# Threshold attention and a bilinear feed-forward layer: five more units of weights turned on TensorE

## The chip, the cores and the metric

The kernel runs on one core of a Trainium2 chip. The metric is the device time of one execution in microseconds (us); less is better. The time before is the median of three runs. A profiled execution, taken by the hardware profiler, shows every instruction of the engines: PE (TensorE's matmuls; PEld its weight loads), DVE (VectorE), ACT (ScalarE), POOL (GpSimd) and SP (SyncE, which issues nearly all DMAs here). Each engine works through its own instructions strictly in the order in which the program has them.

## What is computed

Attention over 8 batches of 8 heads, 576 rows and 64 columns a head, in which only scores within `tau` of their row's maximum count; the heads are put side by side to 4608 rows of 512, and these go through a bilinear layer with 1536 hidden columns.

```python
scores = scale * np.matmul(q, k.transpose(0, 1, 3, 2))
thresh = np.max(scores, axis=-1, keepdims=True) - tau
scores = np.where(scores >= thresh, scores, -1000000000.0)
scores = scores - np.max(scores, axis=-1, keepdims=True)
attn = np.exp(scores)
attn = attn / (np.sum(attn, axis=-1, keepdims=True) + 1e-09)
x = np.matmul(attn, v)                  # (B,H,S,D) -> (B*S, H*D)
out = (x @ w_a) * (x @ w_b) @ w_out
```

All of it is in float32, for which TensorE makes two passes for each matmul; the profile counts passes.

## The kernel before, in words

**Units and slots.** Heads are taken in pairs: a batch has four pairs (0 to 3). A unit `(i, u)` is 128 rows of scores for each head of pair `i` (u = 0 to 3), or, with u = 4 (`NT`), the 64 rows left over of each head, for two neighbouring pairs together. Batch 0 has 18 units: eight of the first half ((0,0) to (3,0), (0,1) to (3,1)), then ten of the second half: 8 = (0,2), 9 = (0,3), 10 = (0,4), 11 = (1,2), 12 = (1,3), 13 = (2,2), 14 = (2,3), 15 = (2,4), 16 = (3,2), 17 = (3,3). There are 144 units in all. The main loop (line 991) has one slot `g` for each, and all instructions of a slot are written out in a fixed order, kept by `keep_order`.

**What a slot does for its unit.** `scores` (line 374): 8 matmuls into two pairs of PSUM banks (line 388), the row maxima on DVE (395) and a threshold (396). `weigh` (406): exponentials on ACT (415, 416), then on DVE the masking with row sums (419); after that the two pairs of banks are free. `reciprocal` (424): while weights are still being converted, the 1e-9 is added on ACT (428) and DVE takes the reciprocal (432).

**Turning.** The products with v need the weights with keys on the partitions. Up to unit 7 (`BY_PE = 8`) TensorE does it: ACT writes two diagonal matrices of reciprocals (`diagonals`, 446), and in the next slot `turn_pe` multiplies the weights, piece by piece, by the diagonals (463; 18 matmuls with 128 moving columns), into two pairs of banks, from which ACT (465) and DVE (466) copy to `wT`. The product (`weighted_unit`) follows two slots after the scores. From unit 8 on ACT scales the weights (`normalise`, 438), DVE turns 32x32 blocks (`turn_blocks`, 482), SP's queue writes them to a DRAM tile `swap` and reads them back in another order into `wT` (`turn_back`, 505), and the product (`weighted`, 590) follows three slots after the scores (`PV_LAG`), for two units of a pair at once. Because the blocks lie in another order, v of batch 0 is loaded a second time (line 1088).

**Feed-forward work.** When a half of 256 rows is complete for all pairs, a generator (`ffn`, line 739) gives its matmuls (691, 764 and 821 or 867) in small steps; `advance(cols)` puts so many columns of them into a slot at fixed places. The speed is set by `PACE`, or by what is left until the next half arrives (line 1012). Each product of a hidden block and w_a or w_b fills a pair of banks (`pab`); ACT copies the first out (770), DVE multiplies the second in (772).

**PSUM.** There are four pairs of banks (`banks`, line 128) for scores, turned weights (`tp`), products with v (`pv`) and the feed-forward layer (`pab`, `po`). A matmul that takes a pair of banks waits until the engine that read its former content is done.

**Weight conversion.** The weights of the layer arrive as 64-bit words. Up to slot 15 each slot converts two or three pieces: ACT (288, 289), POOL (295), then a slot later DVE (301, 309) and POOL (314). In DVE's order one conversion follows the maxima, and one or two follow the reciprocal; in ACT's order the pair 288, 289 of the slot's first piece comes ahead of line 428.

Of the kernel before, what the change touches and what calls it, by code (L numbers as in the profile page):

```python
# [22 lines left out]
PV_LAG = 3  # L23
BY_PE = 8
# [30 lines left out]
def kernel(  # L55
# [411 lines left out]

    def parts(i, u):

        if i < HP:  # L470
            return {1: [(i, 0)], 3: [(i, 1)], NT: [(i, 2), (i + 1, 2)]}.get(u, [])
        return {1: [(i, 0)], NT if i % 2 == 0 else 3: [(i, 1)]}.get(u, [])
# [117 lines left out]
    def weighted(i, h):  # L590
# [4 lines left out]
        if h < 2:  # L595
            groups = G + (n > HALF)
            wT = [turned.pop((i, 2 * h + y))[:, 0:groups] for y in range(2)]
        else:
            t = turned[i - i % 2, NT]
            wT = [t[:, i % 2 * 2 + y:i % 2 * 2 + y + 1] for y in range(2)]  # L600
            if i % 2:
                del turned[i - 1, NT]
        pv = product([lambda rows, s, t=t: t[rows, :, s] for t in wT], loaded[i]["v"], n)
# [374 lines left out]

    def convert_rest(g, k):

        for n in early.get(g - 1, [])[k:k + 1]:
            convert_sign(n)
            convert_shift(n)
            convert_add(n)

    n = 0
# [4 lines left out]
    for g in range(len(units) + PV_LAG):  # L991
# [7 lines left out]
        back = ()  # L999
        if BY_PE + 1 < g <= len(units) + 1:  # L1000
            n = g - PV_LAG
            back = (1 if BY_PE <= n and parts(*units[n]) else 0,)
            if not back[0]:
                turn_back(*units[g - 2])
# [5 lines left out]
        pace = (PACE if g > BY_PE else PACE_EARLY) * BLOCK_COLS  # L1010
        if g > BY_PE:
            pace = min(pace, backlog() / (min([a for a in arrivals if a > g] + [len(units) + PV_LAG + 1]) - g))
        pace += NSLOT * S / (2 * NT + 1) + CATCH_UP * max(backlog() - BLOCK_COLS, 0)
        if 2 <= g < BY_PE + 2:
            weighted_unit(*units[g - 2])
            running["owed"] -= NSLOT * P // 2
# [12 lines left out]
        if g > BY_PE:  # L1029
            advance(PORTIONS[0] * pace)  # L1030
        for p in range(HP, NPR):
            for name, d in (("q0", 1), ("q1", 1)):
                if g == (second if name == "q1" else first)[p] - d - (name == "q1" and p % 2):
                    prep(p, name)
        if here:
            weigh(i, u)
        if here and g < BY_PE:
            reciprocal(i, u, nc.vector)
        if 0 < g <= BY_PE:
            turn_pe(*units[g - 1])  # L1040
        if g < 3:
            prep_copy(*prep_pe(g + 1, "k"))
# [4 lines left out]
        if g > BY_PE:  # L1047
            n = g - PV_LAG
            held = 0.0
            now = parts(*units[n]) if BY_PE <= n < len(units) else []  # L1050
            if now:
                held = 384 - (PORTIONS[2] + PORTIONS[3]) * pace + NSLOT * sum(width(*x) for x in now) // 2
                held = min(max(held, 0.0), 384)
            advance(PORTIONS[1] * pace - held)
            for p, h in now:
                if pairs[p][1] == 0:
                    make_x(2 if h == 1 and p >= HP and pairs[p][0] % GT == 0 else 1)
                make_room()
                weighted(p, h)
                passed(NSLOT * width(p, h) // 2)  # L1060
                running["owed"] -= NSLOT * width(p, h) // 2
            if back and back[0] > 0:
                turn_back(*units[g - 2])
# [3 lines left out]
        if here and g < BY_PE:  # L1067
            diagonals(i, u)
        elif here:
            reciprocal(i, u, nc.scalar if converting else nc.vector)  # L1070
            normalise(i, u)
        convert_rest(g, 1)
        if g <= BY_PE:
# [13 lines left out]
        if BY_PE <= g < BY_PE + HP:  # L1087
            load_v(g - BY_PE, again=True)
        store(written)
        if g > BY_PE:  # L1090
# [58 lines left out]
```

## Time and profile before

| | before |
|---|---|
| median of three runs | 1430.13 us (1428.39 to 1431.39) |
| span of the profiled execution | 1425.2 us |
| PE busy | 1369.9 us (96%), 34208 passes |
| DVE busy | 1007.7 us (71%) |
| ACT busy | 679.4 us (48%) |
| POOL busy | 480.7 us (34%) |

The span is the time from the first to the last instruction of the profiled execution. The page of the profile cuts it into 40 equal slices of 35.6 us; each digit is the busy share of a slice in tenths, PEclk the granted clock of TensorE:

```profile
PE   6778999999999999999999999999999999999998
DVE  6899887788777877776767767677777776744323
ACT  5787554545445454545444545454545455431010
PEclk9999999999999999999999999999999999999999
```

PE is below nine tenths in the first four slices alone (0 to 142 us), where DVE is at its busiest. The groups of instructions that the change touches, with busy us and the mean of one in ns, then the idle time of their engine just before them:

```profile
L438 ACT ACTIVATE tw<-tw,rcp 128x576 f32<-128x576 f32 x272 | 196.1, 768 | 198.1 <-DVE rcp L432 198.1
L482 DVE STREAM_TRANSPOSE tw<-tw 128x576 f32<-128x576 f32 x272 | 194.4, 752 | 0.8 <-ACT tw L438 0.8
L526 PE MATMUL pv<-wT,vm 64*64 64x160 f32 (+3 forms) x5184 | 170.8, 274 | 6.8 <-DMA wT<-swap 3.3
L465 ACT COPY wT<-tp x16: 575/589/599, 22.5 to 83.0; 128x512 f32<-128x512 f32 x16
```

The last line, from the view of one line's instructions, gives the shortest, the median and the longest of them in ns, and when the first and the last began.

### The profile page before, as it was taken

The numbers are of one execution on the slowest core, as the hardware profiler recorded it, in microseconds if no ns is written. First come the engines' busy times: TensorE is split into PE (matmuls) and PEld (weight loads), VectorE is DVE, ScalarE is ACT, GpSimd is POOL, SyncE is SP. The second block draws the span as 40 slices with busy tenths as digits, with TensorE's granted clock in tenths as the row PEclk, the third lists the DMA queues.
The fourth block names the chain that finished last, engine by engine and source line by source line (L and its number), as shares of the span: only waits on it lengthen the run. The fifth ranks groups of instructions, "written<-read, shape, count | busy, mean of one in ns | idle before, by whom it ended". The sixth has DMA issues, their size and how long they took to land.

```text
span 1425.2 us, 76956 instructions
## 1 busy us (share of the span) xinstructions
PE 1369.9 (96%) x34208; PEld 1237.2 (87%) x34208; DVE 1007.7 (71%) x2196; ACT 679.4 (48%) x1244; POOL 480.7 (34%) x668
## 2 busy tenths in 40 slices
PE   6778999999999999999999999999999999999998
PEld 5677689999978887988999989988898899799998
DVE  6899887788777877776767767677777776744323
ACT  5787554545445454545444545454545455431010
POOL 2674541606060605042333323241515060605000
PEclk9999999999999999999999999999999999999999
DMA  9977785667657775666546766567655775550000
GB/s 208 230 220 200 173 220 156 183 146 199 183 141 185 185 184 151 177 156 183 142 130 152 186 171 175 132 174 181 183 135 145 194 196 151 131 151 18 3 18 17
DMA packets 327003, 223.25 MB, mean 157 GB/s; under 512 B 171536, under 2 KB 310800, under 8 KB 326672
## 3 DMA queue, kind: packets, MB, share of 16 engines
q1 hardware_dynamic: 324160, 217.74, 59.6%
q8 instruction: 269, 4.41, 1.4%
q10 hardware_dynamic: 2512, 0.59, 0.2%
q14 instruction: 62, 0.51, 0.1%
HBM read 128.58 MB, written 89.65 MB: 153 GB/s over the span
## 4 chain that ended last, share of the span: by engine, by line
PE 83%; DVE 6%; DMA 5%; SPq 3%; issue 2%; ACT 1%; DVEq 0%; ACTq 0%
PE pab L691 27%; PE po L821 21%; PE pab L764 17%; PE pv L526 10%; PE sc L388 9%; SPq L143 2%; DVE mx L395 1%; DVE tw L482 1%; DMA vm<-in_v_dram 1%; DMA wT<-swap 1%; DVE tw L419 1%; DMA qT<-in_q_dram 1%; DMA sums_u<-in_moe_w_b_dram 1%; DMA raw<-in_moe_w_a_dram 1%; SPq L266 0%
## 5 line engine op out<-in xcount | busy, mean ns | idle before, releaser
L395 DVE TENSOR_REDUCE mx<-sc 128x1 f32<-128x576 f32 x288 | 204.6, 752 | 128.4 <-PE sc L388 127.4
L438 ACT ACTIVATE tw<-tw,rcp 128x576 f32<-128x576 f32 x272 | 196.1, 768 | 198.1 <-DVE rcp L432 198.1
L416 ACT ACTIVATE tw<-sc,bias,scalars 128x576 f32<-128x576 f32 x288 | 239.6, 832 | 10.9 <-DMA qT<-in_q_dram 0.4
L657 POOL TENSOR_TENSOR h<-h,u 128x512 f32<-128x512 f32 x28 | 35.1, 1274 | 605.2 <-DVE h L734 425.8
L419 DVE SCALAR_TENSOR_TENSOR tw<-sc,thr,tw 128x576 f32<-128x576 f32 x288 | 221.4, 799 | 10.0 <-ACT tw L416 9.3
L821 PE MATMUL po<-wo_sb,h 64*64 64x256 f32 x3264 | 208.3, 376 | 1.2 <-DVE h L734 1.1
L482 DVE STREAM_TRANSPOSE tw<-tw 128x576 f32<-128x576 f32 x272 | 194.4, 752 | 0.8 <-ACT tw L438 0.8
L821 PEld LDWEIGHTS po<-wo_sb,h 64*64 64x64 f32 x3264 | 157.7, 133 | 26.5 <-DVE h L734 2.6
L526 PEld LDWEIGHTS pv<-wT,vm 64*64 64x64 f32 x5184 | 160.7, 135 | 19.5 <-issue 11.1
L526 PE MATMUL pv<-wT,vm 64*64 64x160 f32 (+3 forms) x5184 | 170.8, 274 | 6.8 <-DMA wT<-swap 3.3
L388 PE MATMUL sc<-kT,qT 64*64 64x288 f32 x2016 | 168.5, 405 | 2.2 <-DVE xt L534 1.6
L821 PE MATMUL po<-sums_u,h 64*64 64x256 f32 x2448 | 155.1, 376 | 0.7 <-DVE h L772 0.7
L790 POOL TENSOR_TENSOR h<-h 128x256 f32<-128x256 f32 x168 | 117.3, 731 | 107.7 <-PE po L821 102.8
L821 PEld LDWEIGHTS po<-sums_u,h 64*64 64x64 f32 x2448 | 117.2, 133 | 21.3 <-DVE h L772 1.7
L691 PE MATMUL pab<-xU,wb_sb 64*64 64x128 f32 x4096 | 132.6, 269 | 0.0
L691 PEld LDWEIGHTS pab<-xU,wb_sb 64*64 64x64 f32 x4096 | 127.5, 133 | 2.8 <-ACT h L716 0.6
L388 PEld LDWEIGHTS sc<-kT,qT 64*64 64x64 f32 x2016 | 102.2, 134 | 22.8 <-issue 4.9
L415 ACT ACTIVATE bias<-mx,scalars 128x1 f32<-128x1 f32 x288 | 82.8, 287 | 69.0 <-DVE mx L395 68.6
L533 ACT COPY xT<-pv 128x128 f32<-128x128 f32 (+1 forms) x68 | 17.7, 260 | 204.9 <-PE pv L526 204.8
L534 DVE COPY xT<-pv 64x128 f32<-64x128 f32 (+1 forms) x136 | 38.2, 281 | 92.3 <-PE pv L526 90.8
L764 PE MATMUL pab<-xS,wa_sb 64*64 64x256 f32 (+1 forms) x1536 | 99.3, 363 | 0.0
L691 PE MATMUL pab<-xS,wa_sb 64*64 64x128 f32 x2048 | 96.5, 269 | 0.4 <-issue 0.4
(138 smaller groups left out, 2366.2 us busy)
## 6 DMA issues: line engine op xcount, KB each, us to landing
wT<-swap SPq DMA_DIRECT2D x244, 288.0 KB, 4.0
swap<-tw SPq DMA_DIRECT2D x480, 144.0 KB, 3.1
vm<-in_v_dram SPq DMA_DIRECT2D x128, 72.0 KB, 2.3
swap<-tw SPq DMA_DIRECT2D x128, 72.0 KB, 3.0
kT<-in_k_dram SPq DMA_DIRECT2D x112, 72.0 KB, 3.5
wT<-swap SPq DMA_DIRECT2D x56, 144.0 KB, 3.6
out_dram<-kept SPq DMA_DIRECT2D x30, 256.0 KB, 4.1
qT<-in_q_dram SPq DMA_DIRECT2D x112, 40.0 KB, 3.0
```

Of the source, the lines that this page charges most:

```text
L388: nc.tensor.matmul(sc[m][o * D:(o + 1) * D, c], qT[r, q0:q0 + D], kT[r, c * SH:(c + 1) * SH], start=True, stop=True)
L395: nc.vector.tensor_reduce(mx[:, c], sc[j], axis=AX.XY, op=ALU.max)
L415: nc.scalar.activation(bias[:, j:j + 1], mx[:, j:j + 1], AF.Copy, scale=e_nscale)
L416: nc.scalar.activation(wb[j], sb[j], AF.Exp, bias=bias[:, j:j + 1], scale=e_scale)
L419: nc.vector.scalar_tensor_tensor(out=wv, in0=sb[j], scalar=thr[:, j:j + 1], in1=wv, op0=ALU.is_ge, op1=ALU.mult, accum_out=sums[:, j:j + 1])
L438: nc.scalar.activation(w, w, AF.Copy, scale=rcp[:, j:j + 1])
L482: nc.vector.transpose(w, w)
L526: nc.tensor.matmul(pv[c * D:(c + 1) * D, y], vm[rows, s], wT[y](rows, s), start=(s == 0), stop=(s == NSLOT - 1))
L691: nc.tensor.matmul(out[c * D:(c + 1) * D, r, f * P:(f + 1) * P], w[g][k][rows, w0:w0 + D], moving[k][rows], start=(fresh and k == 0 and f ...
L764: nc.tensor.matmul(pab[c * D:(c + 1) * D, r], w[rows, f // n, k, fs + c * D:fs + (c + 1) * D], moving, start=(k == 0), stop=(k == H - 1))
L790: (nc.vector if state["over"] else nc.gpsimd).tensor_tensor(*a, **kw)
L821: nc.tensor.matmul(po[c * D:(c + 1) * D, r, y], ht[rows, t0:t0 + D], other[rows, f], start=(f == 0), stop=(f == NF // 2 - 1))
```

## The change

Units 8 to 12, which are the second halves of pairs 0 and 1 and the leftover rows of both, are turned by TensorE as well. `BY_PE` becomes 13; what began after unit 7 before, and has to do with the feed-forward pace and with `turn_pe` itself, now hangs on a new constant `ALONE = 8`. For these five units ACT writes diagonals in place of scaling the weights, and DVE's transposes, the writes to `swap`, the reads into `wT` and the second load of v for pairs 0 and 1 fall away.

The new `turn_part` takes a unit in two parts, each into one pair of banks that ACT copies out in one instruction (128x640 and 128x512). For an ordinary unit the parts have 8 matmuls with 128 moving columns and 4 with 64, and 8 with 128; for unit 10 they have 20 and 16 with 64. The first part stands after `weigh`, the second after the second portion of feed-forward work. `place` says where a piece lies in `wT`, and `turned_of` hands the product its columns.

The products of units 8 to 12 come two slots after the scores and not three (`weigh_out(now)`, in slots 10 to 14), and stand ahead of `weigh` in their slot. The feed-forward pace counts the turning still to come in these slots (`turns`).

```diff
@@ -21,7 +21,9 @@
     return struct.unpack("<f", struct.pack("<I", bits))[0]
 
 PV_LAG = 3
-BY_PE = 8
+ALONE = 8
+BY_PE = 13
+PE_PAIRS = 2
 XT_BUFS = 7
 Q_BUFS = 2
 OSB_BUFS = 4
@@ -465,6 +467,45 @@
             nc.scalar.copy(wT[:, y * NT:(y + 1) * NT], tp[:, y])
         nc.vector.tensor_copy(wT[:, 2 * NT], last[:, 0])
 
+    def place(s, o):
+
+        if s == 2 * NT:
+            return 2 * P + D + o * (2 * P + D) - D
+        if s >= NT:
+            return 2 * (2 * P + D) + (s - NT) * P + o * D
+        return s // 2 * (2 * P + D) + s % 2 * P + o * D
+
+    def turn_part(i, u, n):
+
+        if n == 0:
+            ws, dg = weights.pop((i, u))
+            t = turned_tile()[:, 0:G].rearrange("p g s e -> p (g s e)")
+            turned[i, u] = [t, [w.rearrange("p n e -> p (n e)") for w in ws], dg]
+        t, ws, dg = turned[i, u]
+        c0, width = ((0, 2 * P + D), (2 * (2 * P + D), 2 * P))[n]
+        tp = banks(width, "tp")
+        for s in ((0, 1, 2, 3, 8), (4, 5, 6, 7))[n]:
+            each = [(0, P)] if u < NT and s < 2 * NT else [(0, D), (1, D)]
+            for o, m in each:
+                y, c = divmod(place(s, o) - c0, width)
+                for j in range(2):
+                    w, d = (j, o * D) if u < NT else (o, (j ^ o) * D)
+                    nc.tensor.matmul(tp[j * D:(j + 1) * D, y, c:c + m], ws[w][:, s * D:(s + 1) * D],
+                                     dg[:, w, d:d + m], start=True, stop=True)
+        nc.scalar.copy(t[:, c0:c0 + 2 * width].rearrange("p (y w) -> p y w", y=2), tp)
+        if n:
+            turned[i, u] = t
+
+    def turned_of(t, o=None, c0=0, n=P):
+
+        def columns(rows, s):
+            if o is None:
+                if s < 2 * NT:
+                    return t[rows, place(s, 0):place(s, 0) + P]
+                return t[rows, 0:2 * (2 * P + D)].rearrange("p (y w) -> p y w", y=2)[:, :, 2 * P:]
+            return t[rows, place(s, o) + c0:place(s, o) + c0 + n]
+        return columns
+
     def parts(i, u):
 
         if i < HP:
@@ -592,15 +633,21 @@
         b, hp = pairs[i]
         flush(("v", i), ("wT", i if i >= HP or h < 2 else i - i % 2, h))
         n = width(i, h)
-        if h < 2:
+        if i >= PE_PAIRS and h < 2:
             groups = G + (n > HALF)
             wT = [turned.pop((i, 2 * h + y))[:, 0:groups] for y in range(2)]
+            wT = [lambda rows, s, t=t: t[rows, :, s] for t in wT]
+        elif h < 2:
+            wT = [turned_of(turned.pop((i, 2 * h + y))) for y in range(2)]
         else:
             t = turned[i - i % 2, NT]
-            wT = [t[:, i % 2 * 2 + y:i % 2 * 2 + y + 1] for y in range(2)]
+            if i < PE_PAIRS:
+                wT = [turned_of(t, i % 2, y * Q, Q) for y in range(2)]
+            else:
+                wT = [lambda rows, s, t=t[:, i % 2 * 2 + y]: t[rows, s] for y in range(2)]
             if i % 2:
                 del turned[i - 1, NT]
-        pv = product([lambda rows, s, t=t: t[rows, :, s] for t in wT], loaded[i]["v"], n)
+        pv = product(wT, loaded[i]["v"], n)
         read = [], []
         settled_of[i] = settled_of.get(i, 0) + n
         if settled_of[i] == S:
@@ -976,6 +1023,16 @@
     nc.vector.tensor_tensor(cut, cut, big, op=ALU.add)
     early = {}
 
+    def weigh_out(now):
+
+        for p, h in now:
+            if pairs[p][1] == 0:
+                make_x(2 if h == 1 and p >= HP and pairs[p][0] % GT == 0 else 1)
+            make_room()
+            weighted(p, h)
+            passed(NSLOT * width(p, h) // 2)
+            running["owed"] -= NSLOT * width(p, h) // 2
+
     def convert_rest(g, k):
 
         for n in early.get(g - 1, [])[k:k + 1]:
@@ -996,22 +1053,24 @@
         state["converted"] = state["added"]
         here = g < len(units)
         converting = bool(early.get(g)) or bool(early.get(g - 1))
-        back = ()
+        n = g - (2 if g < BY_PE + 2 else PV_LAG)
+        now = parts(*units[n]) if ALONE <= n < len(units) and not (g >= BY_PE + 2 and n < BY_PE) else []
+        back = False
         if BY_PE + 1 < g <= len(units) + 1:
-            n = g - PV_LAG
-            back = (1 if BY_PE <= n and parts(*units[n]) else 0,)
-            if not back[0]:
+            back = bool(now)
+            if not back:
                 turn_back(*units[g - 2])
         if here:
             i, u = units[g]
             scores(i, u)
             passed(S)
         exchange_blocks()
-        pace = (PACE if g > BY_PE else PACE_EARLY) * BLOCK_COLS
-        if g > BY_PE:
-            pace = min(pace, backlog() / (min([a for a in arrivals if a > g] + [len(units) + PV_LAG + 1]) - g))
+        pace = (PACE if g > ALONE else PACE_EARLY) * BLOCK_COLS
+        if g > ALONE:
+            turns = max(BY_PE - g + 1, 0) * NSLOT * P
+            pace = min(pace, (backlog() + turns) / (min([a for a in arrivals if a > g] + [len(units) + PV_LAG + 1]) - g))
         pace += NSLOT * S / (2 * NT + 1) + CATCH_UP * max(backlog() - BLOCK_COLS, 0)
-        if 2 <= g < BY_PE + 2:
+        if 2 <= g < ALONE + 2:
             weighted_unit(*units[g - 2])
             running["owed"] -= NSLOT * P // 2
         if g < 3:
@@ -1026,51 +1085,53 @@
         load_weights(RAWS)
         if g > BY_PE and g <= len(units):
             turn_blocks(*units[g - 1])
-        if g > BY_PE:
+        if g > ALONE:
             advance(PORTIONS[0] * pace)
+        if g < BY_PE + 2:
+            weigh_out(now)
         for p in range(HP, NPR):
             for name, d in (("q0", 1), ("q1", 1)):
                 if g == (second if name == "q1" else first)[p] - d - (name == "q1" and p % 2):
                     prep(p, name)
         if here:
             weigh(i, u)
-        if here and g < BY_PE:
+        if here and g < ALONE:
             reciprocal(i, u, nc.vector)
-        if 0 < g <= BY_PE:
+        if 0 < g <= ALONE:
             turn_pe(*units[g - 1])
+        elif ALONE < g <= BY_PE:
+            make_room()
+            turn_part(*units[g - 1], 0)
+            running["owed"] -= 5 * P
         if g < 3:
             prep_copy(*prep_pe(g + 1, "k"))
         for p in range(HP, NPR):
             for name, d in (("k", 2),):
                 if g == (second if False else first)[p] - d:
                     prep(p, name)
-        if g > BY_PE:
-            n = g - PV_LAG
+        if g > ALONE:
             held = 0.0
-            now = parts(*units[n]) if BY_PE <= n < len(units) else []
-            if now:
+            if now and g >= BY_PE + 2:
                 held = 384 - (PORTIONS[2] + PORTIONS[3]) * pace + NSLOT * sum(width(*x) for x in now) // 2
                 held = min(max(held, 0.0), 384)
             advance(PORTIONS[1] * pace - held)
-            for p, h in now:
-                if pairs[p][1] == 0:
-                    make_x(2 if h == 1 and p >= HP and pairs[p][0] % GT == 0 else 1)
+            if g >= BY_PE + 2:
+                weigh_out(now)
+            if back:
+                turn_back(*units[g - 2])
+            if g <= BY_PE:
                 make_room()
-                weighted(p, h)
-                passed(NSLOT * width(p, h) // 2)
-                running["owed"] -= NSLOT * width(p, h) // 2
-            if back and back[0] > 0:
-                turn_back(*units[g - 2])
+                turn_part(*units[g - 1], 1)
+                running["owed"] -= 4 * P
         for n in early.get(g, [])[:1]:
             convert_first(n)
             convert_clamp(n)
-        if here and g < BY_PE:
-            diagonals(i, u)
-        elif here:
-            reciprocal(i, u, nc.scalar if converting else nc.vector)
-            normalise(i, u)
+        if here:
+            if g >= ALONE:
+                reciprocal(i, u, nc.scalar if converting else nc.vector)
+            (diagonals if g < BY_PE else normalise)(i, u)
         convert_rest(g, 1)
-        if g <= BY_PE:
+        if g <= ALONE:
             advance(pace)
         convert_rest(g, 2)
         for n in early.get(g, [])[1:]:
@@ -1084,10 +1145,10 @@
         for p in range(1, NPR):
             if g == first[p] - 1:
                 load_v(p)
-        if BY_PE <= g < BY_PE + HP:
-            load_v(g - BY_PE, again=True)
+        if PE_PAIRS <= g - ALONE < HP:
+            load_v(g - ALONE, again=True)
         store(written)
-        if g > BY_PE:
+        if g > ALONE:
             if held:
                 owed, running["owed"] = running["owed"], 0.0
                 advance(held)
```

## The prediction

> **What bounds the kernel now.** I read the span in large stretches first, then slot by slot (a slot runs from one unit's first score matmul, line 388, to the next one's), then the instructions of the slots that the change touches. All times count from the start of the profiled span.
>
> The stretches (columns: length, then busy us and instructions of PE, PEld, DVE, ACT, POOL, then granted clock, DMA share, GB/s):
>
> ```profile
> 88.16:159.31 71.15, 63.02 (x1585) 53.70 (x1581) 66.34 (x144) 52.22 (x102) 41.45 (x42) 0.98 0.78 199
> 159.31:209.14 49.83, 45.71 (x844) 35.59 (x843) 39.28 (x88) 25.47 (x46) 23.16 (x15) 0.97 0.80 200
> 209.14:1253.57 1044.43, 1032.89 (x26207) 929.64 (x26201) 771.56 (x1694) 516.32 (x931) 347.68 (x518) 1.00 0.64 167
> ```
>
> From 209 us on PE is busy 1032.9 of 1044.4 us at full clock: the kernel is matmul-bound there, and one us of matmul added or of idle removed earlier shifts the end by one us. Slots 9 to 17 (88.16 to 159.31) are different: DVE is busy 66.3 of 71.2 us, PE 63.0. These are the slots in which the change works.
>
> What a slot costs PE at its best I take from undisturbed rows: 8 score matmuls 0.97 us; 32 passes with 128 moving columns 0.87, with 256 columns 1.73; a product of line 526 with 64, 128 or twice 32 columns 1.2, 1.96, 2.1; the 36 passes of line 463 2.19. Slots 24 and 25 last 9.41 and 7.01 us and add up to 9.41 and 7.02, so the prices hold. Slots 9 to 22 then lose, as duration less sum, 1.9, 4.5, 2.1, 0, 2.6, 0.9, 0.4, 0, 1.0, 4.0, 0.7, 1.0, 0.1, 1.0: 20.1 us. That is all there is to win here.
>
> PE about slot 10, the largest loss:
>
> ```profile
> 96.58 1.20 PE L388 MATMUL sc<-kT,first_u 64*64 64x288 f32 x16
> 101.35 0.61 PE L764 MATMUL pab<-xT,wa_sb 64*64 64x128 f32 x15
> 104.43 1.33 PE L764 MATMUL pab<-xT,wa_sb 64*64 64x128 f32 x17 [2.48 <-issue]
> 167.45 3.52 PE L526 MATMUL pv<-wT,vm 64*64 64x32 f32 x144 [2.51 <-DMA wT<-swap]
> 103.98:107.40 3.42, 2.97 (x56) 2.97 (x59) 3.42 (x10) 2.15 (x5) 1.12 (x2) 0.50 1.07 322
> ```
>
> The first idle stretch ends when DVE has read the scores and their pair of PSUM banks comes free; the second waits for a turned block from DRAM. After the first, the clock is granted at 0.50 for 3.4 us (last line): 56 passes take 2.97 us that at 27 ns each would take 1.5, so such a window costs 1.4 us.
>
> DVE and ACT there:
>
> ```profile
> 95.53 0.19 ACT L428 ACTIVATE sums<-sums 128x2 f32<-128x2 f32 x1
> 95.75 0.17 DVE L432 RECIPROCAL rcp<-sums 128x2 f32<-128x2 f32 x1
> 95.83 0.69 DVE L301 SCALAR_TENSOR_TENSOR low<-sums_u,low 128x512 uint32<-128x512 uint32 x1
> 97.37 1.51 DVE L309 TENSOR_SCALAR wa_sb<-wa_sb 128x512 uint32<-128x512 uint32 x1
> 99.13 1.41 DVE L395 TENSOR_REDUCE mx<-sc 128x1 f32<-128x576 f32 x2
> 102.11 1.42 DVE L482 STREAM_TRANSPOSE tw<-tw 128x576 f32<-128x576 f32 x2
> 103.46 0.77 DVE L419 SCALAR_TENSOR_TENSOR tw<-sc,thr,tw 128x576 f32<-128x576 f32 x1
> ```
>
> The reader is to see an in-order loop: ACT's line 428 lets DVE take the reciprocal, behind which two weight conversions and the next slot's maxima stand. Whatever makes line 428 late delays all of them.
>
> **The change, part by part.**
> Removed: ten transposes of line 482, a pair 1.35 us (102.11 to 103.46): 6.8 us of DVE in slots 9 to 13. Ten scalings of line 438, a pair 1.4: 7 us of ACT. On SP's queue 24 writes to swap, 10 reads into wT and 8 reloads of v. SP has pauses before 145 us and none from there to 200, and its order from unit 14's writes on is unchanged, so I cost the removed DMAs at nothing.
> Added on ACT: ten diagonals, 0.72 a pair (0.36 each) and ten copies out of PSUM. The row of line 465, 128x512, gives 0.53 each; 128x640 is not in the trace, bounded by 0.53 and by 0.83 (line 416, 576 columns); by columns 0.66. ACT gains about 2.6 us in all: cheap as work. Its place is what counts.
> Added on PE: four units of 16 matmuls with 128 moving columns and 4 with 64, one of 36 with 64. Two passes each: 128 passes at 61 ns (2.19/36) are 7.8 us, 104 passes with 64 columns 3.2 us if half of 61. Their bounds are 17 ns (line 526, 64 columns, quarter tiles) and 61 ns: 9.6 to 14.2 us, I take 11.0. The feed-forward matmuls are the same in number and, by slot 24, in place: up to slot 14 6.5 us of them are put off, and they return in slots 15 to 24. The products of line 526 keep their number and shapes.
>
> So with the same losses the end moves by +11.0; with no loss at all in slots 9 to 22 by 11.0 - 20.1 = -9.1.
>
> **What becomes of the losses.** Two things in the new order count. First, on ACT the copy of a unit's second part stands ahead of that slot's weight conversion and line 428, so DVE's reciprocal now waits for the last turning matmul of its slot. Second, the next first part (or, where one is due, the product with v) takes the banks of a feed-forward product that DVE's line 772 must empty, and that stands behind the reciprocal, the conversions and the maxima. It is a loop through three engines; its pieces all have rows: copy 0.75 with its start, two ACT conversions 1.15, line 428 and reciprocal 0.35, a DVE conversion 0.93, maxima and threshold 1.63, line 772 0.35.
>
> Slot 9 begins as before (88.16): first part after DVE's copy at 91.5, second part done at 95.75, scores 10 at 96.4 (before 96.58).
> Slot 10: from 95.75, 0.75 + 1.15 + 0.35 + 2 x 0.93 + 1.63 + 0.93 + 0.35 = 7.0 brings 102.8; first part 1.25, two half products 1.74, second part 1.0: 106.8; scores 11 at 107.5 (before 107.44).
> Slot 11: again 7.0 to 113.8, product 1.96, the 36-matmul unit 2.2: 118.0; the scores' banks come free after exponentials that now queue behind the product's copies: scores 12 at 119.1 (before 115.94).
> Slot 12: copies out at 119.55, then 1.15 + 0.35 + 0.93 + 1.63 + 0.93 + 0.35 to 124.9; two tail products through one pair of banks, each with its copies, 2.8; exponential and line 419 before the second part may start (129.8), 1.0, 0.9: scores 13 at 131.7 (before 122.80).
> Slot 13: 131.55, the same 5.35 to 136.9, product 1.74, second part 1.0, 0.9: scores 14 at 140.5 (before 131.88).
> Slot 14: 0.75 + 5.35 and one pair of transposes 1.35 to 147.05; product 1.96, exponential and line 419 2.3: scores 15 at 151.2 (before 138.91).
> That is 12.3 late with 6.5 still owed. Slot 15 I leave at 8.7 (before 8.55): 159.9. From 16 on the slots have more matmul ahead of each wait. The late block of slot 18 landed 15.45 us after its transposes ended (152.0 to 167.45); now they end near 164.8, it lands at 180.2 and is wanted at 179.5: the 2.5 us wait and its clock window shrink to 0.7. Slots 16 to 24 at their best sum to 68.4, so scores 25 come at 159.9 + 68.4 + 0.5 = 228.8 against 218.55, with the same work done: **+10.3**.
>
> On top comes the clock. The loop leaves PE idle for about 3.5, 3.5, 2.5 and 3.0 us in slots 10, 11, 12 and 14, each as long as the 2.48 and 2.51 us that were followed by half clock; four windows at 1.4 are 5.6, part of it inside waits that exist anyway: I take half, 2.8. Sum +13.1.
> [...]
>
> The profiled execution has a span of 1425.2 us, 4.9 under the median 1430.13; I add the sum to the median: **1443.2 us**.
>
> **Rivals.**
> 1. PE fills the idle time (the other side). DVE sets slots 9 to 17; 6.8 us off it shorten them, the added matmuls go into PE's idle time, and slot 18's wait goes. For it: the stretch's 66.3 DVE us, 95% of it. Against it: line 428 behind the second copy. It decides if the losses of slots 9 to 22 fall from 20.1 below 8; at 4, 11.0 - 16.1 = -5: 1425.
> 2. ACT reaches line 428 without waiting for the second part, so slots 9 to 14 last little longer than now; the loop doesn't form, slot 18's 4 us are saved, and of the other losses about a fifth, 3.5: 11.0 - 7.5 = +3.5, 1433.6. For it: ACT is busy only 52 of 71 us.
> 3. The loop with every bound at its upper end: four full windows (5.6), and line 309 held up again as at 97.37 (1.51 where 0.42 is usual, beside POOL) in three slots, 3.3, and 64-column passes at 61 ns, 3.2: 10.3 + 12.1 = +22, 1452.
> 4. The change doesn't do what it says: excluded, the new order shows its matmuls.
>
> **How the numbers follow.** Loop as worked out 0.63, rival 1 0.12, rival 2 0.15, rival 3 0.10. The likeliest's own range is +6 to +18 (no window to four, loop pieces 10% off): 1436 to 1448. To leave out no more than 2 in 10, the range reaches down into rival 2 and up into rival 3: 1432 to 1450. Within 0.2% is 2.9 us either way, about what a measurement of this kernel tells from no change: faster 0.11 (rival 1), same 0.09 (the lower half of rival 2, the weak end of rival 1), slower 0.80.
>
> **What would show it.** Right: line 428 of slots 9 to 12 starts only after the second copy; PE idles over 2 us in slots 10, 11, 12 and 14 until DVE's line 772; granted clock of 0.5 after them; scores 15 near 151, scores 25 near 229; slot 18's wait under 1 us. Wrong: scores 15 before 145, or a PE idle sum under 9 us in slots 9 to 22; then rival 1 or 2 holds.

## The result and the profile after

| | before | after |
|---|---|---|
| median of six runs each | 1429.26 us (1423.04 to 1439.05) | 1452.3 us (1449.33 to 1457.66) |
| ratio | | 1.0158 (95%: 1.0130 to 1.0186) |
| span of the profiled execution | 1425.2 us | 1455.8 us (its run: 1457.66) |
| PE passes | 34208 | 34440 |
| slots 9 to 24, first score matmul of unit 9 to that of unit 25 | 130.39 us | 155.32 us |

The ratio goes by all runs of both kernels, so here and below it differs a little from that of the two medians. The kernel became slower by about 23 us; 1443.2 had been forecast, so the time lies above the range's upper end of 1450. The profiled execution is the longest of the six, 5.4 us over their median. Of its 30.6 us over the span of before, slots 0 to 8 account for -2.8, slots 9 to 24 for +24.9 and the 118 slots after them for +8.5. In other profiled kernels with the same work in those last slots these took 1028.7 to 1036.0 us, against 1035.0 in before and 1043.5 here; the 8.5 lie scattered over them and are taken as this execution's own, not the change's. What has to be explained are the 24.9.

The page of after, span in 40 slices of 36.4 us, tenths busy:

```profile
PE   6777899999999999999999999999999999999998
DVE  6875787778777867786667776777777786644223
PEclk9998999999999999999999999999999999999999
```

The fourth slice (109 to 146 us) is the only one in either kernel whose granted clock is below nine tenths. The costliest groups of after that answer to those of before (busy us, mean ns | idle of the engine before them, and what ended it):

```profile
L440 ACT ACTIVATE tw<-tw,rcp 128x576 f32<-128x576 f32 x262 | 188.8, 768 | 203.0 <-DVE rcp L434 203.0
L523 DVE STREAM_TRANSPOSE tw<-tw 128x576 f32<-128x576 f32 x262 | 187.2, 752 | 0.8 <-ACT tw L440 0.8
L567 PE MATMUL pv<-wT,vm 64*64 64x160 f32 (+3 forms) x5184 | 173.2, 278 | 12.4 <-DVE h L819 9.7
```

What was to be removed is gone: ten scalings (272 to 262, 7.3 us of ACT) and ten transposes (7.2 us of DVE). But the products with v now stand 12.4 us idle, 9.7 of them waiting for DVE's line 819, which empties a feed-forward product; before it was 6.8, with 3.3 for the DMA into wT, and that DMA wait is gone.

PE in slots 9 to 14 of after, some of the turning matmuls and the products (start, us, line, tiles, passes, idle before and what ended it):

```profile
89.43 1.32 PE L493 MATMUL tp<-first_u,tw 128*64 128x128 f32 x24 [0.20 <-DVE xT L575]
102.67 2.40 PE L493 MATMUL tp<-first_u,tw 128*64 128x128 f32 x24 [5.04 <-DVE h L819]
118.05 4.12 PE L567 MATMUL pv<-wT,vm 64*64 64x128 f32 x72 [4.47 <-DVE h L819]
122.10 2.46 PE L493 MATMUL tp<-first_u,tw 128*64 128x64 f32 x72
131.34 1.25 PE L567 MATMUL pv<-wT,vm 64*64 64x32 f32 x72 [2.23 <-DVE h L819]
133.20 2.15 PE L567 MATMUL pv<-wT,vm 64*64 64x32 f32 x72 [0.60 <-DVE xt L575]
135.94 3.92 PE L493 MATMUL tp<-first_u,tw 128*64 128x128 f32 x40 [0.59 <-DVE xt L575]
156.76 3.75 PE L567 MATMUL pv<-wT,vm 64*64 64x128 f32 x72 [2.97 <-DVE h L819]
```

Two things are to be seen. Slots 10, 11, 12 and 14 each have a wait for line 819 (the line that was 772). And the same instructions cost nearly twice as much after the wait of 5.04 us as after one of 0.20: 24 passes of line 493 take 1.32 us at 89.43 and 2.40 at 102.67.

Why line 819 is late, on ACT and then on DVE around slots 10 and 11:

```profile
93.88 0.59 ACT L495 COPY wT<-tp 128x512 f32<-128x512 f32 x1 [0.63 <-PE tp L493]
94.36 0.69 ACT L290 ACTIVATE wb_sb<-sums_u 128x512 f32<-128x512 f32 x1
94.94 0.72 ACT L291 ACTIVATE low<-sums_u 128x512 f32<-128x512 uint32 x1
95.56 0.19 ACT L430 ACTIVATE sums<-sums 128x2 f32<-128x2 f32 x1
109.83 0.59 ACT L495 COPY wT<-tp 128x512 f32<-128x512 f32 x1 [2.41 <-PE tp L493]
111.46 0.20 ACT L430 ACTIVATE sums<-sums 128x2 f32<-128x2 f32 x1
```

```profile
95.79 0.17 DVE L434 RECIPROCAL rcp<-sums 128x2 f32<-128x2 f32 x1 [3.54 <-ACT sums L430]
97.41 1.50 DVE L311 TENSOR_SCALAR wa_sb<-wa_sb 128x512 uint32<-128x512 uint32 x1
98.83 1.41 DVE L397 TENSOR_REDUCE mx<-sc 128x1 f32<-128x576 f32 x2
100.28 0.58 DVE L398 TENSOR_SCALAR thr<-mx,scalars 128x2 f32<-128x2 f32 x1
102.12 0.40 DVE L819 TENSOR_TENSOR h<-h,pab 128x256 f32<-128x256 f32 x1
111.69 0.17 DVE L434 RECIPROCAL rcp<-sums 128x2 f32<-128x2 f32 x1 [7.69 <-ACT sums L430]
```

This is the loop of the prediction, link by link: PE's second part ends, ACT copies it (495), converts two pieces (290, 291), adds 1e-9 (430); only then may DVE, which has stood idle for 3.54 and then 7.69 us, take the reciprocal, and behind it come conversions, maxima and line 819, for which PE's next first part or product waits.

PE's clock in the same stretch, cut where the granted clock changes (length; then busy us of PE, PEld, DVE, ACT, POOL; clock, DMA share, GB/s):

```profile
98.57:101.98 3.41, 0.00 (x0) 0.00 (x0) 3.38 (x6) 2.53 (x5) 2.99 (x4) 1.00 0.71 270
101.98:108.80 6.82, 6.13 (x90) 5.71 (x92) 2.02 (x6) 1.07 (x2) 1.27 (x1) 0.50 0.45 156
115.63:122.46 6.83, 4.41 (x78) 4.08 (x80) 2.55 (x6) 0.22 (x2) 2.35 (x3) 0.50 0.46 80
132.70:139.52 6.82, 5.73 (x110) 5.65 (x112) 2.37 (x8) 3.06 (x7) 0.00 (x0) 0.50 0.01 2
156.59:160.00 3.41, 3.24 (x60) 3.25 (x64) 0.11 (x1) 0.00 (x0) 0.00 (x0) 0.50 0.74 178
```

PE does nothing for 3.41 us and is then at half clock for 6.8 us. Two more stretches of 6.8 us lie about the waits of slots 11 and 12; the fourth, in slot 14, has 3.4. In slots 9 to 24 of before there were two such stretches, 3.4 us each.

### The profile page after: what moved, and what is told of

Its sections match the earlier page's. It is cut to its first block, busy times and chain, and to the rows that moved or that the text cites. A ratio compares the mean times of both kernels' runs of the same rounds, so it can differ in the third digit from the quotient of the medians.

```text
span 1455.8 us, 77343 instructions
## 1 busy us (share of the span) xinstructions
PE 1388.4 (95%) x34440; PEld 1258.0 (86%) x34440; DVE 1005.9 (69%) x2186; ACT 681.7 (47%) x1254; POOL 481.3 (33%) x668
## 4 chain that ended last, share of the span: by engine, by line
PE 85%; DVE 6%; DMA 4%; issue 2%; SPq 2%; ACT 1%; DVEq 0%; ACTq 0%
PE pab L738 26%; PE pab L811 19%; PE po L868 18%; PE pv L567 10%; PE sc L390 9%; PE po L914 1%; DVE mx L397 1%; DMA qT<-in_q_dram 1%; DVE tw L421 1%; PE tp L493 1%; SPq L199 1%; DVE tw L523 1%; DMA raw<-in_moe_w_b_dram 1%; DMA vm<-in_v_dram 1%; DVE low L303 1%
## 5 line engine op out<-in xcount | busy, mean ns | idle before, releaser
L440 ACT ACTIVATE tw<-tw,rcp 128x576 f32<-128x576 f32 x262 | 188.8, 768 | 203.0 <-DVE rcp L434 203.0
L868 PE MATMUL po<-wo_sb,h 64*64 64x256 f32 x3264 | 204.9, 376 | 0.1
L523 DVE STREAM_TRANSPOSE tw<-tw 128x576 f32<-128x576 f32 x262 | 187.2, 752 | 0.8 <-ACT tw L440 0.8
L567 PE MATMUL pv<-wT,vm 64*64 64x160 f32 (+3 forms) x5184 | 173.2, 278 | 12.4 <-DVE h L819 9.7
L868 PEld LDWEIGHTS po<-wo_sb,h 64*64 64x64 f32 x3264 | 162.7, 133 | 19.0 <-DVE h L781 0.6
L868 PEld LDWEIGHTS po<-sums_u,h 64*64 64x64 f32 x2448 | 121.2, 133 | 17.5 <-DVE h L819 3.5
L738 PE MATMUL pab<-xU,wb_sb 64*64 64x128 f32 x4096 | 129.0, 269 | 0.4 <-issue 0.4
L390 PEld LDWEIGHTS sc<-kT,qT 64*64 64x64 f32 x2016 | 102.9, 133 | 19.9 <-issue 2.4
L811 PE MATMUL pab<-xS,wa_sb 64*64 64x256 f32 (+1 forms) x1536 | 95.7, 362 | 0.0
L811 PE MATMUL pab<-xS,wb_sb 64*64 64x256 f32 (+1 forms) x1536 | 95.3, 358 | 0.0
```

What stands on the lines that cost most here:

```text
L390: nc.tensor.matmul(sc[m][o * D:(o + 1) * D, c], qT[r, q0:q0 + D], kT[r, c * SH:(c + 1) * SH], start=True, stop=True)
L440: nc.scalar.activation(w, w, AF.Copy, scale=rcp[:, j:j + 1])
L523: nc.vector.transpose(w, w)
L567: nc.tensor.matmul(pv[c * D:(c + 1) * D, y], vm[rows, s], wT[y](rows, s), start=(s == 0), stop=(s == NSLOT - 1))
L738: nc.tensor.matmul(out[c * D:(c + 1) * D, r, f * P:(f + 1) * P], w[g][k][rows, w0:w0 + D], moving[k][rows], start=(fresh and k == 0 and f ...
L811: nc.tensor.matmul(pab[c * D:(c + 1) * D, r], w[rows, f // n, k, fs + c * D:fs + (c + 1) * D], moving, start=(k == 0), stop=(k == H - 1))
```

## The experiments

Each has before as its partner on the same chip. The medians of before differ between the sets of runs (1421.97 to 1429.26 us), so a time that an expectation names is to be compared by the ratio. "Loss" is the length of slots 9 to 24 less what their PE instructions cost undisturbed: 130.39 - 110.3 = 20.1 us in before, 155.32 - 121.4 = 33.9 in after, where 121.4 has 11.1 for the added matmuls. It is read from one execution each.

**Cutting the loop between ACT and DVE (e1_rcp_dve).** The reciprocal of slots 8 to 13 is taken wholly by DVE, right after the masking.

```diff
-        if here and g < ALONE:
+        if here and g <= BY_PE:
             reciprocal(i, u, nc.vector)
...
-            if g >= ALONE:
+            if g > BY_PE:
                 reciprocal(i, u, nc.scalar if converting else nc.vector)
```

> The changed kernel with one link of the loop cut: in slots 8 to 13 DVE adds the 1e-9 and takes the reciprocal itself, right after the masking, so that it no longer waits for ACT's small instruction behind the second copy. The order on PE is the same. Loop theory: slots 9 to 14 last about 56 us in place of 76.3 (8.3, 9, 8.5, 11, 8.5, 10), no idle stretch of PE over 2.5 us is left in slots 10 and 11, and the time falls to about 1432 (1428 to 1438). Rival (the added matmuls and the waits for banks are the cost, whoever takes the reciprocal): slots 9 to 14 stay over 68 us, the time over 1444.

Measured: 1433.72 us against 1421.97, ratio 1.0076 (1.0049 to 1.0103), where after has 1.0158. Slots 9 to 24 take 141.81 us, 13.5 less than in after, with one half-clock stretch of 3.4 us. No idle stretch of PE in slots 10 and 11 is over 2.45 us, as expected, but slots 9 to 14 take 61.1 us and not 56, and the ratio means 1440 beside a before of 1429, not 1432: less is won than was expected. The reciprocal's group (busy us, mean ns | idle before) in after and in this kernel:

```profile
L434 DVE RECIPROCAL rcp<-sums 128x2 f32<-128x2 f32 x144 | 23.9, 166 | 24.6 <-ACT sums L430 19.9
```

```profile
L434 DVE RECIPROCAL rcp<-sums 128x2 f32<-128x2 f32 x144 | 23.9, 166 | 5.3 <-ACT sums L430 0.4
```

19.9 us of DVE waiting for line 430 become 0.4. The loop is there, and about half of the loss to before is its price, clock included.

**Cutting it between PE and ACT (e2_second_late).** The second part moves behind the reciprocal and the diagonals, so that line 430 no longer stands behind its copy.

```diff
-            if g <= BY_PE:
-                make_room()
-                turn_part(*units[g - 1], 1)
-                running["owed"] -= 4 * P
...
             (diagonals if g < BY_PE else normalise)(i, u)
+        if ALONE < g <= BY_PE:
+            make_room()
+            turn_part(*units[g - 1], 1)
+            running["owed"] -= 4 * P
```

> The changed kernel with the loop cut at another place: the second turning part stands behind the diagonals in the program, so that its copy comes behind the weight conversion, the small instruction for the reciprocal and the diagonals on ACT; nothing else moves, PE's order is the same. Loop theory: as good as cutting it on DVE, 1430 to 1440. Rival (ACT itself is too late, wherever the reciprocal is taken): over 1444, because the next exponentials still stand behind the copy.

Measured: 1432.82 us, ratio 1.0074 (1.0051 to 1.0097); slots 9 to 24 141.14. DVE's wait for line 430 falls from 19.9 to 7.2 us. Another link of the same loop, cut by another edit that leaves every engine its work, gives the same time. That it is a loop and not the length of any one engine's work is shown by this pair. What is left after either cut, about +11, is as much as the turning matmuls' own price: the loss is 20.4 and 19.7 us, about that of before again.

**The matmuls alone (e3_pe_only).** Before, with five units' worth of turning matmuls (18 of 128 columns, 36 passes, in each of slots 9 to 13) into a pair of banks that nobody reads. Nothing is left out.

```diff
+    def spare(g):
+
+        tp = banks(P, "tp")
+        for s in range(NSLOT):
+            for j in range(2):
+                nc.tensor.matmul(tp[j * D:(j + 1) * D, s % 2], first_sb[:, s * D:(s + 1) * D], ident,
+                                 start=True, stop=True)
...
             weigh(i, u)
+        if BY_PE < g <= BY_PE + 5:
+            spare(g)
```

> The kernel before with 18 matmuls of the turning shape (128 rows by 64, 128 moving columns) into a pair of banks that nobody reads in each of slots 9 to 13: 90 matmuls, 180 passes, 11.0 us at 61 ns, with no new link between engines but one more pair of banks in the rotation. Loop theory: added matmuls alone mostly fit into idle time of these slots (they lose 11 us): 0 to +6, 1429 to 1435, no half-clock windows beyond the two before. Rival (the matmuls themselves are the cost, they add to the sum of PE): +11 or more, 1440.

Measured: 1435.9 us, ratio 1.0087 (1.0055 to 1.0118), +12.4 us for 5 x 2.19 = 11 us of matmul. This was a miss: PE's idle time in these slots was expected to take half of it or all. The spare group of slot 11 in this kernel:

```profile
116.90 3.66 PE L454 MATMUL tp<-more_u,first_u 128*64 128x128 f32 x36 [3.90 <-DVE h L780]
```

The pair of banks that it takes is one that DVE has yet to empty, so it makes a wait of its own, 3.90 us, and then runs in part at half clock, 3.66 us instead of 2.19. The other four took 2.19 each. Over slots 9 to 13 PE idles 6.7 us in this kernel and 7.0 in before: matmuls that need a pair of banks themselves hardly went into that idle time.

**The matmuls twice (e10_double_turn).** On top of e1, each turning matmul is issued two times.

```diff
-                    nc.tensor.matmul(tp[j * D:(j + 1) * D, y, c:c + m], ws[w][:, s * D:(s + 1) * D],
-                                     dg[:, w, d:d + m], start=True, stop=True)
+                    for _ in range(2):
+                        nc.tensor.matmul(tp[j * D:(j + 1) * D, y, c:c + m], ws[w][:, s * D:(s + 1) * D],
+                                         dg[:, w, d:d + m], start=True, stop=True)
```

> The kernel with the reciprocal on DVE, with each of the 116 turning matmuls of units 8 to 12 made twice into the same place: another 11 us of PE, nothing else. If the added matmuls are paid in full with the loop cut, the ratio goes from 1.0076 to about 1.015. If they lie in PE's idle time of these slots (12.8 us in slots 9 to 24), it stays under 1.011.

Measured: 1451.72 us against 1426.45, ratio 1.0185 (1.0153 to 1.0218), 0.0109 above e1: some 15 us by the ratios, 10 to 22 by their intervals, and 11.6 us more in slots 9 to 24 of the profiled execution (153.37 against 141.81), for 11 us more of matmul. It takes no new pair of banks and still nothing of it is hidden: PE idles 12.3 us in these slots, 12.8 in e1 and 12.3 in before. By the same numbers the first 11 us weren't hidden either.

**The clock kept up (e5_warm).** After, with matmuls that nobody reads, into unused columns of a pair of banks already held: 72 ahead of slot 10's first part, 36 and 44 ahead of the products of slots 12 and 14.

```diff
+    def keep_warm(rounds):
+
+        for _ in range(rounds):
+            for r in range(2):
+                rows = slice(r * D, (r + 1) * D)
+                for c in range(2):
+                    nc.tensor.matmul(state["open"][c * D:(c + 1) * D, r], first_sb[rows, 0:D], ident[rows],
+                                     start=False, stop=False, skip_group_check=True)
...
         if g < BY_PE + 2:
+            keep_warm({12: 9, 14: 11}.get(g, 0))
             weigh_out(now)
...
+            keep_warm({10: 18}.get(g, 0))
             turn_part(*units[g - 1], 0)
```

> The changed kernel with matmuls that nobody reads (72, 36 and 44 of them, 27 ns a pass, into unused columns of the open pair of banks) where PE idles in slots 10, 12 and 14; the loop and all waits stay. Clock theory (the term that was mis-sized: three windows of half clock of 6.8 us and one of 3.4, about 10 us in all): the granted clock stays 1.0 in slots 10, 12 and 14, these get shorter by about 3.1, 2.8 and 1.7 us, slot 11 stays at 14.8 as the control, and the time falls by 7 to 8, to about 1445. Rival (half clock only fills time that the loop waits anyway): slots 10, 12 and 14 as long as before, 1452.

Measured: 1440.43 us, ratio 1.0127 (1.0096 to 1.0157), against 1.0158 for after; the intervals overlap, so the 4 us between them are likely and not certain, and less than the 7 to 8 expected. The profile is plainer: slots 10, 12 and 14 take 13.1, 13.3 and 10.1 us instead of 15.95, 15.47 and 11.64, and slot 11, which got no such matmuls, 14.3 instead of 14.8. The half-clock stretches of slots 10, 12 and 14 are gone, that of slot 11 stays, at 3.4 us. So some 6.6 us of the three slots were clock; slots 16 to 24 took 72.4 us here and 70.3 in after, which takes back 2 of them in this execution.

**The DVE relief given back (e6_dve_back).** On top of e1, two reductions of 128x576 in each of slots 9 to 13, 7.5 us of DVE in all, in the place of the transposes that the change took out. Nobody reads their result.

```diff
             turn_blocks(*units[g - 1])
+        elif ALONE < g <= BY_PE:
+            for j in range(2):
+                nc.vector.tensor_reduce(scalars[:, 6 + j:7 + j], first_sb[:, 0:S], axis=AX.X, op=ALU.max)
```

> The kernel with the reciprocal on DVE (first run of this study), and in each of slots 9 to 13 two DVE reductions of 128x576 that nobody waits for (0.75 us each), where the removed transposes stood: 7.5 us of DVE work put back. If DVE's relief is worth nothing because other waits set these slots, the ratio to the kernel before stays as without them, 1.008 (1.005 to 1.011). If DVE sets the slots once the loop is cut, they cost their 7.5 us: 1.013.

Measured: 1449.94 us against 1428.72, ratio 1.0165 (1.0132 to 1.0197), 0.0089 or some 13 us above e1 (7 to 19 by the intervals; 11.9 in slots 9 to 24). Once the loop is cut, then, the relief is real and worth at least about its 7.5 us; that later emptying also brings half clock fits it (this kernel has four such stretches in slots 9 to 24, e1 one).

**What else stands in the way.** Three edits on the order of DVE's queue. e4_weigh_first is e1 with the products with v put behind `weigh`, so that DVE's copies out of them stand behind the masking:

```diff
-        if g < BY_PE + 2:
-            weigh_out(now)
...
         if here and g <= BY_PE:
             reciprocal(i, u, nc.vector)
+        if g < BY_PE + 2:
+            weigh_out(now)
```

> The kernel with the reciprocal on DVE, and the products with v of units 8 to 12 behind the exponentials and the masking of their slot and no longer ahead of them. PE's order is the same. If the products' place ahead of the exponentials is what still keeps the score banks full in slots 11, 12 and 14, these three slots (11.7, 12.0 and 9.2 us with the reciprocal on DVE alone) get shorter by 4 to 6 us in all and the ratio falls to about 1.004. If the products only wait for the feed-forward banks, whatever stands behind them, it stays at 1.008.

Measured: 1433.35 us against 1428.72, ratio 1.0040 (1.0021 to 1.0060): some 5 us better than e1, though the intervals overlap; its slots 9 to 24 take 138.53 us, 3.3 less than e1's. The ratio is as expected, the place is not: slots 11, 12 and 14 get 1.9 us shorter together (10.15, 11.65 and 9.23 us) and not 4 to 6, slot 10 gets 1.4 longer, and slots 9, 15 and 16 together 2.7 shorter. So the products' place ahead of the exponentials is not shown to be what kept the score banks full. e8_conv_late adds to e4 that the weight conversion which follows the maxima, ahead of line 819, moves behind the masking from slot 9 on:

```diff
-        convert_rest(g, 0)
+        if g < 9:
+            convert_rest(g, 0)
...
+        if g >= 9:
+            convert_rest(g, 0)
```

> As the run with the products behind the exponentials, and besides, from slot 9 on, the weight conversion that DVE makes between the maxima and the emptying of feed-forward banks comes behind both. Loop theory: what waits for DVE's emptying starts 0.9 to 1.3 us sooner in each of slots 9 to 14, some 4 us in all, ratio 1.001 (0.998 to 1.005). Rival: the added matmuls (11 us) are paid in full whatever the order, 1.008.

Measured: 1433.09 us, ratio 1.0026 (0.9998 to 1.0054); its slots 9 to 24 take 135.10 us. e4 and e8 can't be told apart by their ratios; only the profile's slots are shorter, by 3.4. The same move alone in the kernel before (e9_before_conv_late):

> The kernel before with the same move of DVE's weight conversion alone, behind the masking, from slot 9 on; no unit more is turned on TensorE. If DVE's order is what the losses of slots 9 to 15 hang on, the same 4 us are won here too: ratio 0.997. If DVE's amount of work sets these slots, nothing changes: 1.000.

Measured: 1427.35 us, ratio 0.9999 (0.9975 to 1.0024): worth nothing there. Its profiled execution has 135.53 us for slots 9 to 24, 5.1 more than before's, though the span is only 1.7 us longer. So a few us between two executions' slots, as between e1, e4, e8 and e14, are not certain to be the edit's. And alone in after, with the loop uncut (e13_conv_only):

> The changed kernel, loop uncut (the reciprocal still waits for ACT behind the second copy), with DVE's one weight conversion moved from between the maxima and the emptying of the feed-forward banks to behind the masking, where DVE waits for ACT anyway. Loop theory: the loop gets shorter by one conversion, 0.93 to 1.3 us in each of slots 9 to 14, some 6 us, and more where a half-clock window goes: ratio 1.008 to 1.012 in place of 1.0158. Rival (DVE's order is not what the slots wait for): 1.015 to 1.017.

Measured: 1444.51 us against 1426.45, ratio 1.0126 (1.0097 to 1.0155). That is 4.6 us better than after by the ratios, with overlapping intervals, and lies between the two expectations; about a fifth of the 23 us may have been the conversion ahead of line 819. Its slots 10, 11 and 12 still take 13.3, 12.0 and 17.0 us, the last with a half-clock stretch of 10.24 us.

**All cuts together (e14_all).** e8 and e2 in one.

> All cuts together: the reciprocal on DVE, the products behind the masking, DVE's conversion behind both, and the second part's copy behind the diagonals on ACT. If ACT's order still holds up a slot here, a little better than without the last (1.0026), 0.999 to 1.002, which would be level with the kernel before; if DVE's work and PE's sum are the bound by now, the same 1.0026.

Measured: 1427.47 us against 1426.45, ratio 1.0008 (0.9991 to 1.0025): level with before, as the first expectation has it, though the interval overlaps e8's. Slots 9 to 24 as one stretch, and the reciprocal's group:

```profile
87.60:222.32 134.72, 126.50 (x2861) 99.73 (x2857) 116.67 (x236) 82.39 (x159) 66.55 (x56) 1.00 0.56 144
L434 DVE RECIPROCAL rcp<-sums 128x2 f32<-128x2 f32 x144 | 23.9, 166 | 4.9
```

The granted clock is 1.00 through the whole stretch, and line 434 waits for ACT no more. Of the loss, 134.72 - 121.4 = 13.3 us are left, 6.8 less than in before; that does not cover the 11.1 us of added matmul. By this one execution slots 9 to 24 are 4.3 us longer than in before, by the ratio the kernel is 1 us slower (1.3 faster to 3.6 slower). No version beat the kernel before; by this sum slots 9 to 24 get shorter than in before only if the loss falls below 9.

## Why the prediction was right about the loop and wrong about its size

Right: the direction and the mechanism. Line 430 starts after the second copy in each of slots 9 to 13; PE idles over 2 us until line 819 in the four slots named; slot 18's 2.51 us wait for the block from DRAM is gone (0.07 us idle in all of slot 18). The price of the added matmuls held: in e14, where the clock is 1.00 throughout, the eight groups of line 493 take 11.2 us from their start to the next instruction of PE, against the 11.0 forecast, and there are 232 more passes, as counted. The two times given as signs were missed: the scores of slot 15 came at 161.63 us, not near 151, those of slot 25 at 240.68, not near 229. The first rival, in which PE's idle time takes the added matmuls (1425), is refuted by e3 and e10. The second, in which the loop does not form (+3.5), is refuted by the trace of after; and where the loop was cut by hand, in e1 and e2, about +11 was left and not +3.5, since the losses stayed at about 20.

The slots as forecast (without the clock) and as measured:

| slot | forecast us | measured us | more |
|---|---|---|---|
| 9 | 8.2 | 9.1 | 0.9 |
| 10 | 11.1 | 15.9 | 4.8 |
| 11 | 11.6 | 14.8 | 3.2 |
| 12 | 12.6 | 15.5 | 2.9 |
| 13 | 8.8 | 9.3 | 0.5 |
| 14 | 10.7 | 11.6 | 0.9 |
| 15 | 8.7 | 8.8 | 0.1 |
| 16 to 24 | 68.9 | 70.3 | 1.4 |

The sum of the last column is 14.7; 2.8 had been set down for the clock on top. The failing step is this: "four windows at 1.4 are 5.6, part of it inside waits that exist anyway: I take half, 2.8". Two of its three assumptions were wrong.

A window was taken to be 3.4 us long, as the one at 103.98 of before. Three of the four were twice that (PE stood idle for 0.69, 2.42 and 1.09 us in their first 3.4 us, against 0.45 in that of before and 0.16 in the fourth's; the last section says why this counts), and what lay in them was not some of PE's work but all that the loop does on PE. From the end of the wait to the next scores, slot 10 took 110.42 - 102.67 = 7.75 us where 4.7 were forecast, slot 11's product and unit 4.12 + 2.46 = 6.6 instead of 4.2, slot 12 140.71 - 131.34 = 9.4 instead of 6.8, slot 14 4.9 instead of 4.15: 8.8 us more, against the 2.8. And "half, as part lies inside existing waits" could not hold in a loop, where PE's own matmuls (first part, products, second part) are links: whatever slows them makes the next copy, line 430 and line 819 late as well.

The second term is DVE's link, forecast at 7.0 us from the end of one second part to the next line 819's end. In slot 10 it took from 93.83 to 102.52, 8.7, in slot 11 from 109.78 to 118.00, 8.2; in slot 12 6.7, as forecast (6.9). The 2.9 us are for the most part three executions of line 311, two at 1.50 us (97.41, 113.30) and one at 0.83 (101.37) instead of 0.42, and the threshold at 0.58. I had put the former into the third rival only, though the row at 97.37 of before was printed beside my sum. The remaining 3 of the 14.7 us lie in slots 9, 13 and 15 to 24, a little in each, and were not traced further.

So the third rival named the size, 1452, but not for all its reasons: of its three surcharges the full windows came and were larger than it had them, the held-up line came twice at full length and not three times, and the passes with 64 columns at 61 ns did not come: unit 10's 72 took 2.46 us, part of it at half clock.

What stays open is the 8.5 us of the last 118 slots in that one execution, and how the 13 us of DVE relief, the 12 of the loop and the 11 of the matmuls share their waits: the edits' effects don't simply add up (e4's move brings 5 us after e1, the conversion's move 5 us in after and nothing in before). And that the wait before 104.43 in the kernel before ended with DVE's read of the scores, as the prediction has it, is inferred from DVE's rows; the row of PE itself names "issue".

## What to carry to other kernels

Work moved from a busy engine to one that idles is only cheap if the idle time is not itself a wait for the engine that was to be relieved; here PE idled for banks that DVE had to empty, and the added matmuls were paid in full (in e10 11.6 us for 11). Before putting an instruction into an in-order queue, look at what small step stands behind it (here a 0.2 us addition on ACT behind a copy that waits for PE, for which DVE stood idle 3.54 and 7.69 us with two conversions behind the reciprocal) and follow who waits for that until you are back where you began: if you are, the slot becomes the sum of the links. And price a wait on PE not by its length alone: in these traces waits of over 2 us could be followed by half speed for the next 3.4 or 6.8 us (2.51 us by 3.4 in before, 2.23 by 6.8 in after, 2.45 by none in e1), and in a loop that delays all that follows.

## What the runs showed of the hardware that was not expected

The half-clock stretches come in whole multiples of 3.413 us (3.41 and 6.83 us in before and after, 10.24 in e13) and begin on one grid: in after they start at 101.98, 115.63, 132.70 and 156.59 us, which are 4, 5 and 7 times 3.413 us apart (16 of them in 54.61 us), and those of before at 103.98 and 168.84, 19 times. What sets this length, no run shows. Where a wait falls on the grid then matters: 2.23 us of idle ending at 131.34 were followed by 6.8 us of half clock, 2.45 us ending at 100.04 in e1 by none. Each of the 13 traces can be read window by window of 3.413 us on its own grid. In slots 9 to 24, 23 windows at full clock had 2.03 us or more of PE idle in them, and after every one the clock was halved (six of them in before and after, with 2.03 to 3.41 us); after none of those with 1.99 or less, but for one in e4 (1.05). The 2.45 us of e1 fall into two windows, 0.57 and 1.88. Once at half clock, 24 of the 25 windows with 0.52 us of idle or less were followed by full clock (the other, in e3, had 0.10), none of the 7 with 0.58 or more. By these numbers a loop, which brings waits in window after window, stays at half clock longer than one wait alone: 6.8 us at three of the four waits in after, 3.4 at each of the two of before in these slots. The bounds are read from the rows, not set by an experiment.

DVE's line 311 lasts 1.50 us where POOL's line 316 runs beside it. Of after, POOL:

```profile
96.98 1.65 POOL L316 TENSOR_TENSOR wb_sb<-wb_sb,low 128x512 int32<-128x512 int32 x1 [1.24 <-DVE wb_sb L311]
```

It ends at 98.63, line 311 at 98.91, as if DVE's instruction could only begin in earnest once POOL was through. In the 13 traces, 210 of DVE's instructions of this kind (line 309 in before) began while POOL was at work, and every one ended 0.28 or 0.29 us after POOL's instruction; the other 258 took 0.40 to 0.43 us (before and after have 31 of the former and 41 of the latter). No run took POOL's instruction away, and no row shows what holds line 311 up, so the cause is not shown.
